# Turning q, k and features by row halves into two banks, and summing the tail's keys inside each step, in a Performer attention feeding two mixtures

## The chip, the cores and the metric

One core of one Trainium2 chip runs the whole program. The metric is the device time of one execution in microseconds (us), a median over runs. The engines are TensorE (PE, with its weight loads shown as PEld), VectorE (DVE), ScalarE (ACT), GpSimd (POOL) and SyncE (SP, which issues transfers). Each works through its own instructions in order and waits for others by semaphores.

## The reference

Random-feature attention over 2 batches, 8 heads, 576 tokens and 64 columns a head, then two mixtures of dense products whose cost dwarfs it:

```python
def phi(x):
    proj = np.einsum('bhsd,md->bhsm', x, omega)          # 128 features
    h = proj - np.sum(x * x, axis=-1, keepdims=True) / 2.0
    h = h - np.max(h, axis=-1, keepdims=True)
    return np.exp(h) / np.sqrt(m)
q_p, k_p = phi(q_s), phi(k_s)
kv = np.einsum('bhsm,bhsd->bhmd', k_p, v)
z = np.sum(k_p, axis=2)
num = np.einsum('bhsm,bhmd->bhsd', q_p, kv)
den = np.einsum('bhsm,bhm->bhs', q_p, z)[..., None] + 1e-06
x = (num / den)                                           # to 1152 x 512
for e in range(4):                                        # first mixture
    out += p[:, e:e + 1] * (np.maximum(x @ w1[e], 0.0) @ w2[e])
h = out @ w_in                                            # second mixture
return (h * np.cos(h)) @ w_out
```

## The kernel before

Attention is worked off in steps `s`, one for each of the 8 pairs of heads of one batch. A step has 512 tokens a head: four tokens lie on each of the 128 partitions, so a head is four tiles of 128 tokens. The last 64 tokens of every head and batch are kept apart as the "tail" (`kL`, `qL`, `veL`, features `phiL`): batch 0 on partitions 0 to 63, batch 1 on 64 to 127.

The steps are a software pipeline, written out by hand in the loop over `s`; there is no scheduler, so each engine's order is the order of the code. In one step TensorE does, in this order: the rest of `nums(s-2)` (tile `num`: features of q times kv, 128x64 weights, two column halves side by side); `kv_of(s-1)` (features of k times v, written into a free corner of a `num` bank, so its rows read `num<-ve,phk`); `turn_ahead(s)` (turns q of step s and k of step s+1, `tp_q` and `tp_k`, four 128x128 turns each); `turn_phi(s-1)` (turns the features of q, `tq`, eight turns); the products with omega for q and for k (`pj_q`, `pj_k`, in two row halves side by side); and the turn of the finished attention rows (`tx`). From step 6 on quanta of the dense products (`g`) are put between `tx` and `num`. Everything after about 84 us is dense products.

VectorE copies `xT_q` and half of the turned features `pT` out of PSUM, takes the maxima of `pj` (`three_q`, `three_k`), divides (`rd`, `xs`) and adds the tail's part to kv (`kv<-num,kvL`, L1172). ScalarE copies `xT_k` and the other half of `pT` and does all exponentials (`phq`, `phk`, L1092). The tail's keys times values are made once, in step 1, by `kv_tail`: 32 small products in four banks (`kvL`), copied out by VectorE in four pieces of 128x260.

PSUM has eight banks, all from one pool. Tiles of a step reuse the banks of earlier ones: a product must wait until the readers of its bank's last tile are done. `pj_k` of a step waits in this way for the division and the kv addition of the same step.

Of the kernel before, what the change touches and what calls it, by code (L numbers as in the profile page):

```python
# [9 lines left out]
F32 = mybir.dt.float32  # L10
# [16 lines left out]
def performer_moe_kernel(ctx, tc, q, k, v, omega, probs, w1, w2, w_in, w_out, out):  # L27
    nc = tc.nc
# [921 lines left out]
    with tc.tile_pool(name="at1", bufs=1) as at1, tc.tile_pool(name="at2", bufs=2) as at2:  # L950
# [76 lines left out]
        def turn(nm, t, pieces=1):  # L1027

            n = R // pieces
            tps = []  # L1030
            for z in range(pieces):
                tp = bank(f"tp_{nm}_{z}")[:, : n * P]
                tps.append((slice(z * n * P, (z + 1) * n * P), tp))
                for i in range(n):
                    nc.tensor.transpose(
                        tp[:, i * P : (i + 1) * P], t[:, 2 * (z * n + i) : 2 * (z * n + i) + 2, :], ident
                    )

            def copy(x=None, x2=None, act=nm[0] == "k"):
                if x is None:  # L1040
                    x = at2.tile([P, R * P], F32, tag=f"xT{nm[0]}", name=f"xT_{nm}")
                for z, (c, tp) in enumerate(tps):
                    if act and z == 0:
                        nc.scalar.activation(x[:, c], tp, ACTF.Copy)
                    else:
                        nc.vector.tensor_copy(out=x[:, c], in_=tp)
                    if x2 is not None:
                        nc.scalar.activation(x2[:, c], tp, ACTF.Square)
                return x

            return copy

        def features(nm, turned, phi, squares=None, shift_later=False):
# [35 lines left out]
            for g, pj in enumerate(pjs):  # L1089
                for i in range(4):  # L1090
                    ix = g + 2 * i
                    nc.scalar.activation(  # L1092
                        phi[:, ix, :], pj[:, i * M : (i + 1) * M], ACTF.Exp, bias=nb[:, ix : ix + 1]
                    )
                yield

        def divide(nm, parts):

# [39 lines left out]
        kvL = at1.tile([P, H, B, D + 1], F32, name="kvL")  # L1138
# [6 lines left out]
        def kv_tail(phi):  # L1145
            for z in range(2):
                hs = range(z * H // 2, (z + 1) * H // 2)
                sums_ = [
                    bank(f"kvL_{z}_{b}")[:, : H // 2 * (D + 1)].rearrange("p (h e) -> p h e", e=D + 1) for b in range(B)
                ]  # L1150
                for n, h in enumerate(hs):
                    for c in (slice(0, P // 2), slice(P // 2, P)):
                        for b in range(B):
                            bl = slice(b * L, (b + 1) * L)
                            nc.tensor.matmul(
                                sums_[b][c, n, :], phi[bl, h, c], veL[bl, h, :], start=True, stop=True
                            )
                for b in range(B):
                    nc.vector.tensor_copy(out=kvL[:, hs.start : hs.stop, b, :], in_=sums_[b])

        def kv_of(i):
            b, hp = pairs[i]
            ve, phk = ves[i % 2], phks.pop(i)
            kvp = room.pop() if room else bank(f"kv_{i}")
            kvp = kvp[:, 4 * (D + 1) : 6 * (D + 1)].rearrange("p (h e) -> p h e", h=2)
            for h in range(2):
                for r in range(R):
                    column_halves(
                        kvp[:, h, :], phk[:, h * R + r, :], ve[:, h * R + r, :], r == 0, r == R - 1
                    )  # L1170
            yield
            nc.vector.tensor_tensor(out=kv[hp][:, :, b, :], in0=kvp, in1=kvL[:, 2 * hp : 2 * hp + 2, b, :], op=ALU.add)  # L1172

        pTs = {}
        room = []

        def turn_phi(i):
            phq = phqs[i]
            for h in range(2):
                tp = bank(f"tq_{i}_{h}")  # L1180
                for r in range(R):
                    nc.tensor.transpose(tp[:, r * P : (r + 1) * P], phq[:, h * R + r, :], ident)
                pT = at2.tile([P, R * P], F32, tag=f"pT{h}", bufs=1, name=f"pT_{i}_{h}")
                if h == 0 and i:
# [3 lines left out]
                pTs[i, h] = pT  # L1188

        def nums(i):  # L1190
            b, hp = pairs[i]
            xss[i] = xs = at2.tile([P, R, 2, D], F32, tag="xs", bufs=1, name=f"xs_{i}")
            parts = []
            for h in (1, 0):
                pT = pTs.pop((i, h))
                num = bank(f"num_{i}_{h}")
                for r in range(R):
                    column_halves(
                        num[:, r * (D + 1) : (r + 1) * (D + 1)], pT[:, r * P : (r + 1) * P], kv[hp][:, h, b, :]
                    )  # L1200
# [4 lines left out]
            divide(i, parts)  # L1205

        def tail_turn_phi():
            phq = phqs[NPR]
            for g in range(2):
                tp = bank(f"tqL_{g}")  # L1210
                for i in range(4):
                    nc.tensor.transpose(tp[:, i * P : (i + 1) * P], phq[:, 4 * g + i, :], ident)
                pT = at2.tile([P, R * P], F32, tag=f"pT{g}", bufs=1, name=f"pTL_{g}")
                if g == 0:
                    nc.scalar.activation(pT, tp, ACTF.Copy)
                else:
                    nc.vector.tensor_copy(out=pT, in_=tp)
                pTs[NPR, g] = pT

        def tail_nums():  # L1220
            xss[NPR] = xs = at2.tile([P, NP, 2, D], F32, tag="xs", bufs=1, name="xsL")
            parts = []
            for z in range(2):
                num = bank(f"numL_{z}")
                for n in range(H // 2):
                    hp, h = divmod(z * H // 2 + n, 2)
                    for b in range(B):
                        bl = slice(b * L, (b + 1) * L)
                        nc.tensor.matmul(
                            num[bl, n * (D + 1) : (n + 1) * (D + 1)],  # L1230
                            pTs[NPR, z][:, n * P + b * L : n * P + (b + 1) * L],
                            kv[hp][:, h, b, :], start=True, stop=True,
                        )
                parts.append((num, xs.rearrange("p n h d -> p (n h) d")[:, z * 4 : z * 4 + 4, :]))
# [54 lines left out]
            return qL if s == NPR else qts[s]  # L1289

        def turn_ahead(s, act=True):
            splits = []
            if s <= NPR:
                splits.append((("q", s), turn(f"q{s}", q_of(s))))
            if s + 1 < NPR:
                splits.append((("k", s + 1), turn(f"k{s + 1}", kts[s + 1])))
# [52 lines left out]
        for s in range(NPR + 3):  # L1349
# [4 lines left out]
            else:  # L1354
# [111 lines left out]
```

## Time and profile before

| | |
|---|---|
| median of 3 runs | 640.69 us (640.3 to 640.7) |
| the profiled execution's own time | 640.93 us |
| its span, first to last instruction | 639.2 us |
| TensorE busy | 633.7 us, 99% |
| VectorE / ScalarE / GpSimd busy | 76% / 55% / 27% |
| granted clock of TensorE | 1.00 throughout |

TensorE is named busy nearly all of the time, but its matmuls are pipelined and their ends are modelled, so "busy" also covers short waits between them. The shares of the other engines are averages over two unlike parts: 84 us with attention, and 555 us of dense products.

### The profile page before, as it was taken

How to read it: one execution, taken by the hardware profiler on the slowest of the kernel's cores; microseconds unless marked ns; L12 is line 12 of the kernel's file. 1: busy time of each engine (PE TensorE's matmuls, PEld its weight loads, DVE VectorE, ACT ScalarE, POOL GpSimd, SP SyncE). 2: the span in 40 equal slices, each digit the busy share in tenths (PEclk: the TensorE clock that was granted, in tenths of full speed). 3: DMA queues.
4: the chain of work that ended last, by engine and by line, in shares of the span. 5: the costliest groups of instructions: out<-in, count | busy, mean ns of one | idle time of the engine just before them, and what ended most of it. 6: DMA issues, size and time to landing. Idle time of an engine off the chain costs nothing.

```text
span 639.2 us, 10046 instructions
## 1 busy us (share of the span) xinstructions
PE 633.7 (99%) x3751; PEld 538.0 (84%) x3751; DVE 488.5 (76%) x878; ACT 352.8 (55%) x686; POOL 173.8 (27%) x218
## 2 busy tenths in 40 slices
PE   8999999999999999999999999999999999999997
PEld 7999989988888888888888888888888888888887
DVE  5998578789688688598687697699698772697842
ACT  6898664365346454354443455544457973476821
POOL 7899752033332333323333232310000000000000
PEclk9999999999999999999999999999999999999999
DMA  7645430313446434347424445401250002500111
GB/s 166 188 118 149 133 100 31 102 67 131 133 148 200 146 106 143 128 148 217 134 98 132 138 130 209 132 35 70 85 208 33 2 0 91 239 1 2 49 50 49
DMA packets 55440, 70.95 MB, mean 111 GB/s; under 512 B 15200, under 2 KB 40032, under 8 KB 55392
## 3 DMA queue, kind: packets, MB, share of 16 engines
q1 hardware_dynamic: 46800, 40.92, 20.5%
q0 software_dynamic: 8448, 29.37, 13.5%
q8 instruction: 29, 0.48, 0.3%
q14 instruction: 19, 0.16, 0.1%
q10 hardware_dynamic: 144, 0.03, 0.0%
HBM read 55.36 MB, written 14.94 MB: 110 GB/s over the span
## 4 chain that ended last, share of the span: by engine, by line
PE 97%; DVE 1%; DMA 1%; SPq 0%; issue 0%; DVEq 0%
PE g L779 46%; PE g_odd L585 4%; PE g L549 3%; PE g_1c L549 2%; PE g_0a L549 2%; PE g_3a L549 2%; PE g_2a L549 2%; PE g_1a L549 2%; PE g_3c L549 2%; PE g_2c L549 2%; PE g_0c L549 2%; PE num L1143 2%; PE pj_q L1062 1%; PE g_0d L549 1%; PE g_0b L549 1%; PE g_3e L549 1%
## 5 line engine op out<-in xcount | busy, mean ns | idle before, releaser
L749 ACT ACTIVATE sth<-h 128x512 fp32r<-128x512 f32 (+1 forms) x111 | 60.3, 555 | 80.3 <-PE g L779 66.4
L258 POOL TENSOR_TENSOR c<-c 128x512 uint32<-128x512 uint32 x32 | 46.9, 1467 | 84.6 <-issue 34.2
L752 DVE SCALAR_TENSOR_TENSOR stl<-h,sth 128x512 fp32r<-128x512 f32 (+1 forms) x72 | 48.9, 694 | 27.1 <-ACT sth L749 26.9
L779 PE MATMUL g<-v3h,sth 128*128 128x512 f32 (+1 forms) x110 | 42.9, 390 | 0.0
L779 PE MATMUL g<-v0h,sth 128*128 128x512 f32 (+1 forms) x110 | 42.7, 388 | 0.0
L779 PE MATMUL g<-v1h,sth 128*128 128x512 f32 (+1 forms) x110 | 42.7, 388 | 0.0
L779 PE MATMUL g<-v2h,stl 128*128 128x512 f32 (+1 forms) x110 | 42.5, 387 | 0.0
L779 PE MATMUL g<-v2h,sth 128*128 128x512 f32 (+1 forms) x110 | 42.5, 386 | 0.0
L779 PE MATMUL g<-v0h,stl 128*128 128x512 f32 (+1 forms) x110 | 42.4, 386 | 0.0
L779 PE MATMUL g<-v3l,sth 128*128 128x512 f32 (+1 forms) x110 | 42.4, 386 | 0.0
L779 PE MATMUL g<-v3h,stl 128*128 128x512 f32 (+1 forms) x110 | 42.4, 386 | 0.0
L779 PE MATMUL g<-v1h,stl 128*128 128x512 f32 (+1 forms) x110 | 42.4, 385 | 0.0
L779 PE MATMUL g<-v1l,sth 128*128 128x512 f32 (+1 forms) x110 | 42.4, 385 | 0.0
L779 PE MATMUL g<-v0l,sth 128*128 128x512 f32 (+1 forms) x110 | 42.4, 385 | 0.0
L779 PE MATMUL g<-v2l,sth 128*128 128x512 f32 (+1 forms) x110 | 42.4, 385 | 0.0
L293 DVE TENSOR_TENSOR stl<-h,sth 128x512 fp32r<-128x512 f32 (+1 forms) x39 | 22.8, 594 | 19.3 <-ACT sth L749 19.1
L451 DVE SCALAR_TENSOR_TENSOR c<-c 128x512 f32<-128x512 f32 (+1 forms) x38 | 25.0, 662 | 11.9 <-ACT c L449 11.7
L448 ACT ACTIVATE c<-h 128x512 f32<-128x512 f32 x32 | 19.9, 621 | 19.8 <-DVE h L626 19.8
L805 DVE SCALAR_TENSOR_TENSOR acc<-g,pn,acc 128x512 f32<-128x512 f32 x27 | 20.1, 745 | 6.7 <-PE g L779 6.7
L779 PEld LDWEIGHTS g<-v2h,stl 128*128 128x128 f32 x110 | 20.7, 188 | 4.5 <-DVE stl L752 0.4
L779 PEld LDWEIGHTS g<-v0h,stl 128*128 128x128 f32 x110 | 20.7, 188 | 4.3 <-DVE stl L752 0.2
L779 PEld LDWEIGHTS g<-v3h,stl 128*128 128x128 f32 x110 | 20.7, 188 | 4.2
(427 smaller groups left out, 1880.5 us busy)
## 6 DMA issues: line engine op xcount, KB each, us to landing
rv<-in_moe_w_dram SPq DMA_DIRECT2D x16, 512.0 KB, 3.9
c<-in_moe_w_in_dram POOLq DMA_DIRECT2D x16, 512.0 KB, 4.1
c<-in_moe_w_out_dram POOLq DMA_DIRECT2D x16, 512.0 KB, 3.9
kt<-in_k_dram SPq DMA_DIRECT2D x8, 256.0 KB, 3.5
qt<-in_q_dram SPq DMA_DIRECT2D x8, 256.0 KB, 4.0
ve<-in_v_dram SPq DMA_DIRECT2D x16, 128.0 KB, 4.0
ra_2as<-in_moe_w_dram SPq DMA_DIRECT2D x8, 256.0 KB, 3.3
out_dram<-acc SPq DMA_DIRECT2D x7, 256.0 KB, 2.3
```

The source lines that it names most:

```text
L258: nc.gpsimd.tensor_tensor(out=total, in0=t, in1=lw, op=ALU.add)
L293: nc.vector.tensor_tensor(out=dst, in0=x, in1=y, op=ALU.subtract)
L448: nc.scalar.activation(vv, src, ACTF.Copy, bias=0.25, scale=INV_2PI)
L451: nc.vector.scalar_tensor_tensor(out=vv, in0=kk, scalar=ROUND, in1=vv, op0=ALU.subtract, op1=ALU.subtract)
L549: nc.tensor.matmul(dst, x[:, o], y[:, kk], start=start and n == 0, stop=stop and n == 3 * kn - 1, skip_group_check=reopen,)
L585: nc.tensor.matmul(g, x[:, kk], w[:, :, :, kk, :], start=n == 0, stop=n == 3 * KD - 1)
L749: nc.scalar.activation(hi, src, ACTF.Relu if self.e < E else ACTF.Copy)
L752: nc.vector.scalar_tensor_tensor(out=to, in0=src, scalar=0.0, in1=hi.bitcast(F32), op0=ALU.max, op1=ALU.subtract)
L779: nc.tensor.matmul(g, x, y[:, o : o + w], start=n == 0, stop=n == 3 * FT - 1)
L805: nc.vector.scalar_tensor_tensor(out=acc[t], in0=src, scalar=p_, in1=acc[t], op0=ALU.mult, op1=ALU.add)
L1062: nc.tensor.matmul(pj[:, i * M : (i + 1) * M], x_[r, c], y[r, :], start=z == 0, stop=z == (squares is not None),)
L1143: nc.tensor.matmul(dst[c], weights[:, c], moving, start=start, stop=stop)
```

## The change

Four things change. `turn_ahead` and `turn_phi` no longer turn whole 128x128 tiles. The new `row_halves` turns partitions 0 to 63 and 64 to 127 of each tile by two instructions (64 rows by 128 columns of weights, 64 moving columns) that write into two banks; each bank then holds one row half of all tiles, so both q and k, and both heads, need both banks' copies. One copy is VectorE's, the other ScalarE's (both VectorE's where only q is turned). `kv_tail` and its copies are gone: `kv_of` adds the tail's product for a head as a fifth term behind the four of the step, so that kv's addition becomes a plain copy. The exponentials of the tail's features are reordered so that heads 0 and 1 come first. `nums` and `tail_nums` take their weights from the new layout.

```diff
+        def row_halves(dsts, srcs):
+            for n, src in enumerate(srcs):
+                for z, dst in enumerate(dsts):
+                    r = slice(z * D, (z + 1) * D)
+                    nc.tensor.transpose(dst[:, n * D : (n + 1) * D], src[r], ident[r, r])
...
                 for r in range(R):
-                    column_halves(
-                        kvp[:, h, :], phk[:, h * R + r, :], ve[:, h * R + r, :], r == 0, r == R - 1
-                    )
-            yield
-            nc.vector.tensor_tensor(out=kv[hp][:, :, b, :], in0=kvp, in1=kvL[:, 2 * hp : 2 * hp + 2, b, :], op=ALU.add)
+                    column_halves(kvp[:, h, :], phk[:, h * R + r, :], ve[:, h * R + r, :], r == 0, False)
+                column_halves(kvp[:, h, :], phiL[bl, n, :], veL[bl, n, :], False, True)
+            yield
+            nc.vector.tensor_copy(out=kv[hp][:, :, b, :], in_=kvp)
...
         def turn_phi(i):
-            phq = phqs[i]
-            for h in range(2):
-                tp = bank(f"tq_{i}_{h}")
-                for r in range(R):
-                    nc.tensor.transpose(tp[:, r * P : (r + 1) * P], phq[:, h * R + r, :], ident)
+            tps = [bank(f"tq_{i}_{z}") for z in range(2)]
+            row_halves(tps, [phqs[i][:, n, :] for n in range(2 * R)])
...
-            for key, split in splits:
-                turned[key] = split(act=act and key[0] == "k")
+            n = len(parts) * R
+            tps = [bank(f"tp_{s}_{z}")[:, : n * D] for z in range(2)]
+            row_halves(tps, [t[:, 2 * i : 2 * i + 2, :] for _, t in parts for i in range(R)])
+            x = at2.tile([P, 2 * R * P], F32, tag="xT", name=f"xT_{s}")
+            to = x[:, : n * P].rearrange("p (i z t) -> p i z t", z=2, t=D)
+            for z, tp in enumerate(tps):
+                src = tp.rearrange("p (i t) -> p i t", t=D)
+                if z and act and n > R:
+                    nc.scalar.activation(to[:, :, z, :], src, ACTF.Copy)
+                else:
+                    nc.vector.tensor_copy(out=to[:, :, z, :], in_=src)
...
                 if s == 1:
                     turn_phi(0)
-                    kv_tail(phiL)
                     next(kvs, None)
```

How TensorE's order moves from kv to the turns, in the middle of step 3. Before (`ve` and `phk` are v and the features of k, `qt` and `kt` q and k as loaded, `ident` the unit matrix):

```order
L1143 MATMUL num_1_633<-ve_131,phk_432 64x65 [waits DMAHW0_49]
L1143 MATMUL num_1_633<-ve_131,phk_432 64x65 x7
L1143 MATMUL num_1_633<-ve_131,phk_432 64x65 [waits DMAHW1_49]
L1143 MATMUL num_1_633<-ve_131,phk_432 64x65 x7
L1035 MATMUL tp_q_0_677<-ident,qt_3_504 128x128 [waits DMAHW7_49]
L1035 MATMUL tp_q_0_677<-ident,qt_3_504 128x128 x3
L1035 MATMUL tp_k_0_682<-ident,kt_0_502 128x128 [waits DMAHW6_49,DVE_49,Activation_49]
L1035 MATMUL tp_k_0_682<-ident,kt_0_502 128x128 x3
```

The same place on TensorE in the changed kernel, up to the first turns:

```order
L1148 MATMUL num_1_630<-ve_131,phk_410 64x65 [waits DMAHW0_49]
L1148 MATMUL num_1_630<-ve_131,phk_410 64x65 x7
L1148 MATMUL num_1_630<-veL,phiL 64x65 x2
L1148 MATMUL num_1_630<-ve_131,phk_410 64x65 [waits DMAHW1_49]
L1148 MATMUL num_1_630<-ve_131,phk_410 64x65 x7
L1148 MATMUL num_1_630<-veL,phiL 64x65 x2
L1143 MATMUL tp_0_678<-ident,qt_3_482 128x64 [waits DMAHW7_49,PE_49]
L1143 MATMUL tp_1_679<-ident,qt_3_482 128x64 [waits DVE_49,Activation_49]
```

Each head's eight products are now followed by two of the tail, which use 64 rows of weights where their neighbours use 128; and the turns of q alternate between two banks, as those of k behind them do.

VectorE in step 1, before (`pT` are the turned features of q, `kvL` the tail's part, `three` the maxima):

```order
L1187 COPY pT_1_388<-tq_1_383 128x512 [waits PE_49]
L1159 COPY kvL<-kvL_0_390 128x4x65 [waits PE_49]
L1159 COPY kvL<-kvL_1_391 128x4x65 [waits PE_49]
L1159 COPY kvL<-kvL_0_410 128x4x65 [waits PE_49]
L1159 COPY kvL<-kvL_1_411 128x4x65 [waits PE_49]
L1172 TENSOR_TENSOR kv_138<-kv_359,kvL 128x2x65 [waits DVE_49]
L1069 TENSOR_REDUCE three_q_455<-x_q_287 128x8 [waits Pool_49]
```

The same place on VectorE in the changed kernel:

```order
L1175 COPY pT_0_404<-tq_0_386 128x512 [waits PE_49]
L1175 COPY pT_1_406<-tq_1_387 128x512 [waits PE_49]
L1162 COPY kv_138<-kv_365 128x2x65
L1069 TENSOR_REDUCE three_q_433<-x_q_286 128x8 [waits Pool_49]
L1075 TENSOR_REDUCE three_q_433<-pj_q_0_412 128x4 [waits PE_49]
```

The four copies of `kvL` are gone, and what was an addition to kv is a copy.

## Rows read from the trace of the kernel before

**Rows 1.** The page, part 1: busy us (share of the span) x instructions.

```profile
PE 633.7 (99%) x3751; PEld 538.0 (84%) x3751; DVE 488.5 (76%) x878; ACT 352.8 (55%) x686; POOL 173.8 (27%) x218
```

**Rows 2.** Busy time of each engine by stage; window, its length, then each engine.

```profile
core 0: us, PE busy (x) PEld busy (x) DVE busy (x) ACT busy (x) POOL busy (x), PEclk, DMA share, GB/s
...
21.60:49.40 27.80, 27.80 (x475) 25.20 (x472) 26.86 (x87) 26.65 (x89) 25.12 (x36) 1.00 0.53 145
49.40:84.00 34.60, 34.55 (x410) 32.16 (x409) 22.34 (x67) 26.47 (x71) 29.12 (x32) 1.00 0.42 121
84.00:639.00 555.00, 551.81 (x2562) 462.98 (x2558) 425.29 (x688) 286.23 (x486) 102.77 (x120) 1.00 0.32 106
```

**Rows 3.** The chain that ended last, one step: start us, us, what.

```profile
28.37 0.59 PE tp_q L1035 x4
28.96 0.44 PE tp_k L1035 x4
29.40 0.90 PE tq L1182 x8
30.30 1.09 PE pj_q L1062 x16
31.39 1.06 PE pj_k L1062 x16
32.45 0.59 PE tx L1116 x4
33.04 2.02 PE num L1143 x64
```

**Rows 4.** Timeline, one turn of the loop: start us, us, engine, line, out<-in.

```profile
29.10 0.68 DVE L1046 COPY xT_q<-tp_q 128x512 f32<-128x512 f32 x1
...
30.38 0.76 DVE L1108 TENSOR_TENSOR xs<-num,rd 128x256 f32<-128x256 f32 x2
...
31.05 0.28 DVE L1172 TENSOR_TENSOR kv<-num,kvL 128x130 f32<-128x130 f32 x1
...
31.29 1.16 PE L1062 MATMUL pj_k<-ws,xT_k 64*128 64x128 f32 x16
...
32.38 0.66 PE L1116 MATMUL tx<-ident,xs 128*128 128x128 f32 x4
...
32.97 1.15 PE L1143 MATMUL num<-kv,pT 128*64 128x65 f32 x32
...
33.95 1.10 PE L1143 MATMUL num<-ve,phk 128*64 128x65 f32 x32
...
34.99 0.66 PE L1035 MATMUL tp_q<-ident,qt 128*128 128x128 f32 x4
...
35.70 0.68 DVE L1046 COPY xT_q<-tp_q 128x512 f32<-128x512 f32 x1
```

**Rows 5.** Timeline: the kv addition and `pj_k`, three loops later.

```profile
51.29 0.28 DVE L1172 TENSOR_TENSOR kv<-num,kvL 128x130 f32<-128x130 f32 x1
...
51.53 1.16 PE L1062 MATMUL pj_k<-ws,xT_k 64*128 64x128 f32 x16
```

**Rows 6.** Timeline of step 1.

```profile
16.30 2.17 ACT L1092 ACTIVATE phk<-pj_k,nb_k 128x128 f32<-128x128 f32 x8
...
17.32 1.43 DVE L1159 COPY kvL<-kvL 128x260 f32<-128x260 f32 x4
```

**Rows 7.** Timeline: the first `num` behind step 1.

```profile
19.62 1.15 PE L1143 MATMUL num<-kv,pT 128*64 128x65 f32 x32
```

**Rows 8.** Timeline, two weight loads of `tp_q`: all four, then the second alone.

```profile
41.81 0.42 PEld L1035 LDWEIGHTS tp_q<-ident,qt 128*128 128x128 f32 x4
...
41.87 0.14 PEld L1035 LDWEIGHTS tp_q<-ident,qt 128*128 128x128 f32 x1
```

**Rows 9.** Timeline of step 7, where only q is turned.

```profile
60.09 0.69 DVE L1046 COPY xT_q<-tp_q 128x512 f32<-128x512 f32 x1 [2.38 <-PE tp_q L1035]
...
62.07 0.66 PE L1116 MATMUL tx<-ident,xs 128*128 128x128 f32 x4
```

More of the change, by code (lines that the diff above doesn't have):

```diff
@@ L1040, in copy @@
                 if x is None:
-                    x = at2.tile([P, R * P], F32, tag=f"xT{nm[0]}", name=f"xT_{nm}")
+                    x = at2.tile([P, R * P], F32, tag=f"xT{nm[0]}", bufs=1 + (nm[0] == "k"), name=f"xT_{nm}")
                 for z, (c, tp) in enumerate(tps):
@@ L1088, in features @@
             yield
[L1089 to L1093, printed above, removed]
-                    )
-                yield
+            order = [g + 2 * i for g in range(2) for i in range(R)]
+            if squares is not None:
+                order.insert(1, order.pop(R))
+            for ix in order:
+                i, g = divmod(ix, 2)
+                nc.scalar.activation(
+                    phi[:, ix, :], pjs[g][:, i * M : (i + 1) * M], ACTF.Exp, bias=nb[:, ix : ix + 1]
+                )
         def divide(nm, parts):
@@ L1143, in column_halves @@
                 nc.tensor.matmul(dst[c], weights[:, c], moving, start=start, stop=stop)
[L1145 to L1159, printed above, removed]
         def kv_of(i):
@@ L1165, in kv_of @@
             kvp = kvp[:, 4 * (D + 1) : 6 * (D + 1)].rearrange("p (h e) -> p h e", h=2)
+            bl = slice(b * L, (b + 1) * L)
             for h in range(2):
+                n = 2 * hp + h
                 for r in range(R):
-                    column_halves(
-                        kvp[:, h, :], phk[:, h * R + r, :], ve[:, h * R + r, :], r == 0, r == R - 1
-                    )
+                    column_halves(kvp[:, h, :], phk[:, h * R + r, :], ve[:, h * R + r, :], r == 0, False)
+                column_halves(kvp[:, h, :], phiL[bl, n, :], veL[bl, n, :], False, True)
             yield
-            nc.vector.tensor_tensor(out=kv[hp][:, :, b, :], in0=kvp, in1=kvL[:, 2 * hp : 2 * hp + 2, b, :], op=ALU.add)
+            nc.vector.tensor_copy(out=kv[hp][:, :, b, :], in_=kvp)
         pTs = {}
@@ L1177, in turn_phi @@
         def turn_phi(i):
-            phq = phqs[i]
-            for h in range(2):
-                tp = bank(f"tq_{i}_{h}")
-                for r in range(R):
-                    nc.tensor.transpose(tp[:, r * P : (r + 1) * P], phq[:, h * R + r, :], ident)
-                pT = at2.tile([P, R * P], F32, tag=f"pT{h}", bufs=1, name=f"pT_{i}_{h}")
-                if h == 0 and i:
+            tps = [bank(f"tq_{i}_{z}") for z in range(2)]
+            row_halves(tps, [phqs[i][:, n, :] for n in range(2 * R)])
+            for z, tp in enumerate(tps):
+                pT = at2.tile([P, R * P], F32, tag=f"pT{z}", bufs=1, name=f"pT_{i}_{z}")
+                if z and i:
                     nc.scalar.activation(pT, tp, ACTF.Copy)
@@ L1187, in turn_phi @@
                     nc.vector.tensor_copy(out=pT, in_=tp)
-                pTs[i, h] = pT
+                pTs[i, z] = pT
         def nums(i):
@@ L1194, in nums @@
             for h in (1, 0):
-                pT = pTs.pop((i, h))
                 num = bank(f"num_{i}_{h}")
                 for r in range(R):
-                    column_halves(
-                        num[:, r * (D + 1) : (r + 1) * (D + 1)], pT[:, r * P : (r + 1) * P], kv[hp][:, h, b, :]
-                    )
+                    for z in range(2):
+                        nc.tensor.matmul(
+                            num[z * D : (z + 1) * D, r * (D + 1) : (r + 1) * (D + 1)],
+                            pTs[i, z][:, (h * R + r) * D : (h * R + r + 1) * D],
+                            kv[hp][:, h, b, :], start=True, stop=True,
+                        )
                 parts.append((num, xs[:, :, h, :]))
@@ L1207, in tail_turn_phi @@
         def tail_turn_phi():
[L1208 to L1218, printed above, removed]
+            turn_phi(NPR)
         def tail_nums():
@@ L1230, in tail_nums @@
                             num[bl, n * (D + 1) : (n + 1) * (D + 1)],
-                            pTs[NPR, z][:, n * P + b * L : n * P + (b + 1) * L],
+                            pTs[NPR, b][:, (z * 4 + n) * L : (z * 4 + n + 1) * L],
                             kv[hp][:, h, b, :], start=True, stop=True,
@@ L1291, in turn_ahead @@
         def turn_ahead(s, act=True):
-            splits = []
-            if s <= NPR:
-                splits.append((("q", s), turn(f"q{s}", q_of(s))))
+            parts = [(("q", s), q_of(s))] if s <= NPR else []
             if s + 1 < NPR:
-                splits.append((("k", s + 1), turn(f"k{s + 1}", kts[s + 1])))
-            for key, split in splits:
-                turned[key] = split(act=act and key[0] == "k")
+                parts.append((("k", s + 1), kts[s + 1]))
+            if not parts:
+                return
+            n = len(parts) * R
[3 more added lines that the diff above has]
+            to = x[:, : n * P].rearrange("p (i z t) -> p i z t", z=2, t=D)
+            for z, tp in enumerate(tps):
+                src = tp.rearrange("p (i t) -> p i t", t=D)
[3 more added lines that the diff above has]
+                    nc.vector.tensor_copy(out=to[:, :, z, :], in_=src)
+            for j, (key, _) in enumerate(parts):
+                turned[key] = x[:, j * R * P : (j + 1) * R * P]
         def k_features(s, shift_later=False):
```

1 line of the change is left out of this document (removed).

## The prediction

> **What bounds the kernel now.** I read the page first: TensorE is named busy for 99% of the span [rows 1]. The busy times by stage say where the change can matter: behind 84 us TensorE has 551.81 us of work in 555, and between 49.4 and 84 us 34.55 in 34.60, so whatever the attention steps shift arrives at the end undiminished [rows 2]. From 21.6 to 49.4 us it is otherwise: TensorE 27.80, VectorE 26.86, ScalarE 26.65, GpSimd 25.12 of 27.80. Four engines are all but full, so a saving on one of them is not yet a saving of time. The chain that ended last names TensorE alone there [rows 3], and taken at its word the turns (0.59 + 0.44 + 0.90 us a step) are on the path. But the chain follows one releaser where two come together. The timeline shows the second: VectorE's copy `xT_q` at 29.10 starts an unbroken series on VectorE (copy, small reductions, `xs`, the kv addition) that ends at 31.05 + 0.28 = 31.33, and `pj_k` starts at 31.29. Then TensorE runs `tx`, `num`, kv and `tp_q` with no more than the changes of shape between them, and `xT_q` of the next step starts at 35.70, when `tp_q` at 34.99 + 0.66 has ended [rows 4]. That is a closed loop of 6.60 us: 2.19 on VectorE, 1.09 for `pj_k`, 0.59 `tx`, 0.98 `num`, 1.04 kv, 0.71 for the turn of q and its way to VectorE. Three loops later the kv addition ends at 51.57 and `pj_k` starts at 51.53 [rows 5]. So it is tight throughout: `pj_k` needs banks that the division and the kv addition free. What matters in steps 2 to 6 is what the change does to this loop, not to TensorE's work.
>
> **Prices.** A turn of 128x128 costs 0.44 / 4 = 0.11 us. `tp_q`, the same four turns behind a change of tile shape, costs 0.59, and `tx` 0.59 too: 0.15 us for each change of shape. The 32 pairs of column halves of `num` and kv (64 records, two to a matmul) cost 2.02 less one change, 1.87 / 32 = 0.058 us a pair [rows 3].
>
> **The turns.** A pair of row halves moves 64 columns in each half, about what a pair of `num` moves (65), so I price it at 0.058; the bounds are that and 0.11, if the two halves gain nothing on a whole turn. A second weight load of a turn started 0.06 us after the first [rows 8], which sits at the lower bound. For that lower bound against the upper one: the Trainium skill ("TensorE: Matmul & The Clock Gate", section LDWEIGHTS) says that a weight load takes P / 1.2 ns with P the columns, whatever the rows. By it the 128 columns of a half would take an estimated 107 ns, a pair would cost what a turn costs, and the sum below would rise by the 2.8 us of the second rival; the 0.06 us disagrees, and is what I go by.
>
> In the loop the turns gain nothing. Before, VectorE waited for four turns (0.44); now each of the two banks is ready only when all eight pairs of q and k are done, 8 x 0.058 = 0.46: +0.02. The 0.4 us saved on `tq` and the change of shape that falls away ahead of `pj_q` lie beside VectorE's series and ScalarE's copy, which `pj_q` now needs as well.
>
> **The tail inside kv.** For each head two matmuls are added, two pair times, 2 x 0.058 = 0.12; four pairs a step, 0.23. They hold 64 rows of weights among neighbours with 128, so the shape changes into them and out of them for both heads; the last change out was there already. Three changes are new, 3 x 0.15 = 0.45. Together +0.68 a step, on TensorE between `num` and the turns, inside the loop, with nothing beside it. No row shows a change from 128x64 to 64x64; its bounds are 0 and the 0.15 of the changes in [rows 3], and I take 0.15 because it is what both of those cost. Behind this stands the Trainium skill ("TensorEngine Tiling (Array Packing)", section Key Properties): a change of the tiling mode, not of the tile alone, drains TensorE, and it lists 128x64 and 64x64 as different modes. The rows agree for the shapes that they hold; no row has this one.
>
> The kv addition (0.28) becomes a copy. Four copies of 260 took 1.43, 0.36 each [rows 6], so 130 should take between half of that and 0.28: I take 0.23, -0.05.
>
> **Step 1.** The 1.43 us of copies leave VectorE, which is full there, and with them the 32 products of `kv_tail`. But `num` at 19.62 [rows 7] cannot come forward by more than about 1.1: one of its two banks is freed by the exponentials of k's features, which end at 16.30 + 2.17 = 18.47 [rows 6] and do not depend on what changes. Bounds 0 and -1.1; I take -1.0, since TensorE itself would be there by then (the tail's first products wait for two exponentials, which the new order of the features puts first).
>
> **Steps 7 to 9.** TensorE is the bound [rows 2]. Steps 7 and 8 pay the tail's +0.68 each. In step 7 `tx` waits for the series behind `xT_q` [rows 9]: four pairs instead of four turns give back 0.21, two copies of 256 columns instead of one of 512 (0.36 each against 0.69) take 0.03. I count -0.2 for step 7 and -0.1 for step 8. The tail's turn in step 9 saves 0.42 and pays two changes of shape, 0.30: -0.1.
>
> **Sum.** Step 1: -1.0. Steps 2 to 6: 5 x (0.68 + 0.02 - 0.05) = +3.25. Steps 7 and 8: 1.36 - 0.3 = +1.06. Step 9: -0.1. Together +3.2. The profiled execution took 640.93, its span 639.2 and 1.7 around it that doesn't change; the median of the runs is 0.24 lower. 640.93 + 3.2 = 644.1, against the median 640.69 + 3.2 = 643.9. With 0 to -1.1 for step 1 and 0.10 to 0.15 for each of the 21 changes of shape, this case alone spans 642.7 to 644.9.
>
> **Rivals.** First, not slower: going between 128x64 and 64x64 costs nothing, since both write 64 columns side by side. Then 21 x 0.15 = 3.15 falls away and the time is 640.7, no change that can be measured (0.2%, 1.3 us, is about what a measurement of this kernel tells from none). It decides from 0.06 us a change downward, where the sum drops under 1.3. Against it: both changes of shape that can be read off [rows 3] cost the same 0.15, though they come from different shapes (128x64 and 64x128). Second, the change does not do what it says: the halves do not run beside each other, or each is held up by its 128 columns of weights, and a pair costs 0.11. Then the loop's turns take 8 x 0.052 = 0.42 more, 2.1 in steps 2 to 6, with 0.3 in steps 7 and 8 and 0.4 in step 9: 646.7. Against it: the 0.06 us of [rows 8]. Third, faster: the loop through VectorE has slack that the timeline doesn't show, and TensorE's own work decides. Then a step saves 16 x 0.052 = 0.83 on turns and 0.15 on the shape ahead of `pj_q` and pays 0.68: -0.3, five times -1.5; steps 7 and 8 -0.1 each, step 9 -0.1, step 1 -1.1: 637.8. It decides where `pj_k` has 0.95 us (0.65 + 0.3) to spare behind VectorE; [rows 4, 5] leave it none.
>
> **How the numbers follow.** Chances: the forecast 0.62, free changes of shape 0.14, halves without gain 0.12, slack 0.12. Slower by over 0.2%: the forecast and the second rival, 0.74. Within 0.2%: most of the first rival and the shallow end of the third, 0.12. Faster: the rest, 0.14. The forecast's own range holds too little, so the range reaches down to the first rival and up to just short of the second: 640.4 to 646.4.
>
> **What would show it.** Right: the loop from one `xT` copy to the next at about 7.25 us instead of 6.6; kv between `num` and the turns at about 1.7 instead of 1.04, with idle ahead of each tail piece; sixteen row-half turns in about 0.6; `pj_k` still starting where the kv copy ends; the first dense quantum of step 6 about 2.2 later. Wrong: tail pieces that follow their neighbours with no gap; turns at over 0.8 for sixteen; or `pj_k` starting clear of the kv copy.

## The result, and the profile after

The changed kernel takes 644.22 us (median of 6 runs, 643.4 to 644.7) against 640.7 (640.3 to 640.9): a ratio of 1.0054, 95% interval 1.0042 to 1.0067. The profiled execution took 644.21, its span is 642.4 against 639.2. The forecast was 643.9.

The page, part 1, of the changed kernel (answers to [rows 1]):

```profile
PE 634.0 (99%) x3879; PEld 536.9 (84%) x3879; DVE 487.9 (76%) x876; ACT 354.0 (55%) x686; POOL 174.0 (27%) x218
```

Nothing shows here: TensorE has 128 more instructions and 0.3 us more busy time. The stages say more. Windows of the changed kernel; each ends at about the same work as its row in [rows 2], the first begins at the same time:

```profile
core 0: us, PE busy (x) PEld busy (x) DVE busy (x) ACT busy (x) POOL busy (x), PEclk, DMA share, GB/s
21.60:51.50 29.90, 27.98 (x566) 24.44 (x565) 26.45 (x85) 26.13 (x84) 27.04 (x38) 1.00 0.55 152
51.50:87.00 35.50, 34.23 (x464) 31.27 (x462) 21.61 (x69) 26.78 (x71) 26.69 (x28) 1.00 0.32 99
87.00:642.00 555.00, 551.86 (x2562) 463.02 (x2558) 426.53 (x688) 286.34 (x486) 103.37 (x121) 1.00 0.32 106
```

The first stage ends 2.1 us later, and TensorE, busy for 27.80 of 27.80 before, now stands for 1.9 of 29.90. The dense stretch has 551.86 of work, 551.81 before. So nearly the whole loss lies ahead of 87 us. One turn of the loop, from the timeline of the changed kernel in step 3 and the first part of step 4 (answers to [rows 4]):

```profile
29.03 0.69 DVE L1287 COPY xT<-tp 128x512 f32<-128x512 f32 x1 [0.53 <-PE tp L1143]
...
33.89 0.64 PE L1148 MATMUL num<-ve,phk 128*64 128x65 f32 x16
...
34.46 0.33 PE L1148 MATMUL num<-veL,phiL 64*64 64x65 f32 x4
...
34.72 0.69 PE L1148 MATMUL num<-ve,phk 128*64 128x65 f32 x16
...
35.34 0.33 PE L1148 MATMUL num<-veL,phiL 64*64 64x65 f32 x4
...
35.60 0.47 PE L1143 MATMUL tp<-ident,qt 64*128 64x64 f32 x8
...
35.90 0.41 PE L1143 MATMUL tp<-ident,kt 64*128 64x64 f32 x8
...
36.15 0.67 PE L1143 MATMUL tq<-ident,phq 64*128 64x64 f32 x16
...
36.35 0.69 DVE L1287 COPY xT<-tp 128x512 f32<-128x512 f32 x1 [0.63 <-PE tp L1143]
...
37.16 1.00 PEld L1062 LDWEIGHTS pj_q<-ws,xT 64*128 64x128 f32 x16 [0.48 <-ACT xT L1285]
...
37.64 0.76 DVE L1109 TENSOR_TENSOR xs<-num,rd 128x256 f32<-128x256 f32 x2
...
38.31 0.28 DVE L1162 COPY kv<-num 128x130 f32<-128x130 f32 x1
...
38.45 0.72 PEld L1062 LDWEIGHTS pj_k<-ws,xT 64*128 64x128 f32 x9 [0.29 <-DVE xs L1109]
```

From kv's first product to the first turn it takes 35.60 - 33.89 = 1.71, before 1.04 [rows 4]. Behind each tail piece the next work starts 0.26 us later, for two pairs. Eight turns of tiles (sixteen row halves) take 36.15 - 35.60 = 0.55, four pairs of k 0.25, a pair 0.06. And where the lines of [rows 4] have no bracket, three waits of step 4 now stand in brackets: VectorE for the turns (0.63), TensorE for ScalarE's copy of `xT` ahead of `pj_q` (0.48) and for `xs` ahead of `pj_k` (0.29). Ahead of `pj_k` the wait is not the same in every step. In steps 4 and 5 it is for `xs`; in steps 2, 3 and 6 it is for ScalarE's exponentials of k's features (`phk`, 0.46, 0.39 and 0.39), so in these steps the loop runs from the copy of `xT` over VectorE's `nb_k` and these exponentials to `pj_k`. Step 3, from the timeline of the changed kernel:

```profile
31.23 0.97 PEld L1062 LDWEIGHTS pj_k<-ws,xT 64*128 64x128 f32 x16 [0.39 <-ACT phk L1094]
```

Step 1 of the changed kernel, from its timeline (answers to [rows 6, 7]):

```profile
14.28 0.33 PE L1148 MATMUL kv<-veL,phiL 64*64 64x65 f32 x4 [0.55 <-ACT phiL L1094]
...
15.87 2.23 ACT L1094 ACTIVATE phk<-pj_k,nb_k 128x128 f32<-128x128 f32 x8
...
18.21 1.15 PE L1186 MATMUL num<-kv,pT 128*64 128x65 f32 x32
```

`num` starts 1.41 earlier. Further on, the copies of `xT` in steps 6, 7 and 8 and the first product behind the attention (answers to [rows 9] and to 49.33, 60.09, 69.63 and 84.20 before):

```profile
51.58 0.69 DVE L1287 COPY xT<-tp 128x512 f32<-128x512 f32 x1 [0.92 <-PE tp L1143]
...
62.82 0.76 DVE L1287 COPY xT<-tp 128x256 f32<-128x256 f32 x2 [3.43 <-PE tp L1143]
...
72.71 0.76 DVE L1287 COPY xT<-tp 128x256 f32<-128x256 f32 x2 [0.75 <-PE tp L1143]
...
87.20 0.50 PE L779 MATMUL g<-v0h,sth 128*128 128x512 f32 x1
```

Read as lateness against before this is the whole account: -1.41 at `num` of step 1, +2.25 in step 6, +2.73 in step 7, +3.08 in step 8, +3.00 at the dense products, +3.3 at the end (the medians differ by 3.5).

### The profile page after: what moved, and what is told of

Same layout as the page of the kernel before. It is cut to its first block, busy times and chain, and to the rows that moved or that the text cites. A ratio compares the mean times of both kernels' runs of the same rounds, so it can differ in the third digit from the quotient of the medians.

```text
span 642.4 us, 10310 instructions
## 1 busy us (share of the span) xinstructions
PE 634.0 (99%) x3879; PEld 536.9 (84%) x3879; DVE 487.9 (76%) x876; ACT 354.0 (55%) x686; POOL 174.0 (27%) x218
## 4 chain that ended last, share of the span: by engine, by line
PE 94%; DVE 3%; ACT 1%; issue 1%; DVEq 0%; ACTq 0%
PE g L779 44%; PE g_odd L585 4%; PE g L549 3%; PE g_1c L549 2%; PE g_0a L549 2%; PE g_3a L549 2%; PE g_2a L549 2%; PE g_1a L549 2%; PE g_2c L549 2%; PE g_3c L549 2%; PE g_0c L549 2%; PE num L1148 2%; PE num L1186 1%; PE pj_k L1062 1%; PE g_0d L549 1%; PE g_0b L549 1%
```

## The experiments

Each median is over 4 to 11 executions. The first columns are read from the one execution of each kernel that was profiled, from the starts of VectorE's copy of `xT` (of q alone where it is a copy of its own) in steps 2 to 6: four loops. "Dense" is the start of the product that stands at 87.20 above. The start of the first `num` behind step 1 varied within 17.7 to 18.6 in the eleven kernels without the tail's sums in step 1 and within 19.35 to 19.62 in the three with them, so loops are compared and not absolute starts.

| kernel | loops, us | four loops | dense | median, us | ratio to before, 95% |
|---|---|---|---|---|---|
| before | 6.77 6.60 6.81 6.82 | 27.00 | 84.20 | 640.7 to 641.0 | |
| changed | 7.39 7.32 7.62 7.61 | 29.94 | 87.20 | 644.22 | 1.0054 (1.0042 to 1.0067) |
| e1 turns alone | 6.77 6.64 7.06 6.94 | 27.41 | 84.33 | 642.09 | 1.0018 (1.0009 to 1.0026) |
| e2 tail alone | 7.33 7.28 7.50 7.51 | 29.62 | 87.51 | 643.60 | 1.0040 (1.0026 to 1.0053) |
| e3 tail over 128 rows | 6.95 6.88 7.17 7.18 | 28.18 | 84.62 | 641.07 | 1.0005 (0.9996 to 1.0014) |
| e4 tails together | 7.24 7.18 7.47 7.46 | 29.35 | 86.44 | 642.73 | 1.0028 (1.0017 to 1.0039) |
| e5 tq twice | 7.59 7.52 7.62 7.61 | 30.34 | 87.30 | 645.90 | 1.0081 (1.0067 to 1.0095) |
| e6 whole turns, 128 rows | 6.89 6.82 7.06 7.07 | 27.84 | 83.97 | 640.73 | 0.9998 (0.9989 to 1.0007) |
| e7 whole turns of q, k | 7.34 7.26 7.97 7.96 | 30.53 | 87.48 | 644.72 | 1.0062 (1.0048 to 1.0076) |
| e8 kv addition twice | 7.09 6.92 7.00 7.00 | 28.01 | 85.02 | 641.50 | 1.0011 (1.0002 to 1.0020) |
| e9 second head late, 128 rows | 10.27 10.22 10.25 10.23 | 40.97 | 99.58 | 655.70 | 1.0232 (1.0218 to 1.0246) |
| e10 second head late | 9.00 10.34 10.39 10.41 | 40.14 | 99.66 | 657.82 | 1.0258 (1.0242 to 1.0274) |
| e11 whole turns of features | 7.39 7.32 7.41 7.41 | 29.53 | 87.00 | 644.29 | 1.0055 (1.0043 to 1.0068) |
| e12 second head early | 7.72 7.53 7.53 7.52 | 30.30 | 85.78 | 642.98 | 1.0033 (1.0021 to 1.0045) |

**One part alone: e1 and e2.** e1 is the changed kernel with `kv_tail` and the addition back (these lines undone), e2 the kernel before with these alone:

```diff
-                    column_halves(kvp[:, h, :], phk[:, h * R + r, :], ve[:, h * R + r, :], r == 0, r == R - 1)
+                    column_halves(kvp[:, h, :], phk[:, h * R + r, :], ve[:, h * R + r, :], r == 0, False)
+                column_halves(kvp[:, h, :], phiL[bl, n, :], veL[bl, n, :], False, True)
...
-            nc.vector.tensor_tensor(out=kv[hp][:, :, b, :], in0=kvp, in1=kvL[:, 2 * hp : 2 * hp + 2, b, :], op=ALU.add)
+            nc.vector.tensor_copy(out=kv[hp][:, :, b, :], in_=kvp)
...
-                    kv_tail(phiL)
```

> The turns by row halves alone; the tail's part of kv is made once in step 1 and added, as before (q0's and k0's copies share buffers of later steps to make room). Theory (a loop through VectorE sets steps 2 to 6, and eight row-half pairs of q and k, 0.46 us, replace four whole turns, 0.44 us, in it): no gain in the loop (+0.1 in five steps), -0.4 in steps 7 to 9: 640.4 us, 639.9 to 640.9. Rival A (TensorE's own work decides): 0.98 us a step less, five times, and -0.4: about 635.4. Rival B (the copies that now hold q and k together start later or end later than the one of q did, which is why a loop of the changed kernel takes 7.3 to 7.6 us, not 7.25): 0.1 to 0.35 a step more, 640.8 to 642.0.

> The tail inside kv alone (with the new order of the exponentials of its features); turns are whole 128x128 ones, as before. Theory: 7 steps of +0.68 us, less the 1.4 us that step 1 gives back in the changed kernel: 640.7 + 4.8 - 1.4 = 644.1 us (643.5 to 644.6), about what the whole change takes. Rival A (the added products hide beside other engines' work and the turns are what costs): 640.7 less the 1.4 us of step 1, about 639.3 to 640.7.

e2 took 643.60: the tail is nearly all of the loss, with 29.62 - 27.00 = 2.62 in four loops, 0.66 each on the mean. e1, at 642.09, missed the theory's 640.4. It gains nothing in the loop, so TensorE's own work does not decide (635.4 is refuted); it even loses 0.41 in four loops, nearly all of it in the last two (0.25 and 0.12). Rival B was right that something is lost there, though not by the copies of `xT`; e7 and e11 show what it is. At the dense products e1 is only 0.13 late, at the end 1.15. The rest arises at two places behind the attention, 0.4 near 96.6 and 0.66 here. TensorE in the dense stretch of e1, from its timeline:

```profile
100.15 0.50 PE L779 MATMUL g<-v2h,stl 128*128 128x512 f32 x1 [0.57 <-DVE stl L752]
```

VectorE's `stl` comes too late, and TensorE waits 0.57 us; the same product has no such wait before. ScalarE's split of the weights `v3h`, which stands ahead of the activations that `stl` needs, waited in e1 for its load until 81.19, and until 80.06 before. That the one makes the other is read from the order of the work and was not varied by itself, and why the load landed later is open. It need not belong to the turns: the profiled execution of e3 (below) has the same late split (81.23) and the same wait (0.53 at 100.13), and took 642.07, 1.0 above e3's median.

**The price of a change of shape: e3 and e4.** e3 keeps the number of products and their columns, but takes all 128 rows, with zeros for the other batch (to make room, the copies of k's first turns get one buffer instead of two):

```diff
-        veL = at1.tile([P, H, D + 1], F32, name="veL")
+        veLs = [at1.tile([P, H, D + 1], F32, name=f"veL{b}") for b in range(B)]
+        for b, t in enumerate(veLs):
+            nc.vector.memset(t[(1 - b) * L : (2 - b) * L], 0.0)
...
-                column_halves(kvp[:, h, :], phiL[bl, n, :], veL[bl, n, :], False, True)
+                column_halves(kvp[:, h, :], phiL[:, n, :], veLs[b][:, n, :], False, True)
```

e4 sums the tail of head 0 behind its own products and that of head 1 ahead of them, so that both stand together:

```diff
+                if h == 1:
+                    column_halves(kvp[:, h, :], phiL[bl, n, :], veL[bl, n, :], True, False)
                 for r in range(R):
...
-                column_halves(kvp[:, h, :], phiL[bl, n, :], veL[bl, n, :], False, True)
+                if h == 0:
+                    column_halves(kvp[:, h, :], phiL[bl, n, :], veL[bl, n, :], False, True)
```

> The changed kernel with the tail's products over all 128 rows: v of each batch's tail in a copy of its own with zeros in the other batch's rows, so that features of all 128 rows are the weights and no product changes the tile's shape. As many products of the same 65 columns. Theory (three new changes of shape a step at 0.15 us): 7 steps x 0.45 = 3.15 less, 641.1 us (640.5 to 641.7). Rival (changes between 128x64 and 64x64 cost nothing and the products themselves or the longer loop of the copies cost): 644.2, no change.

> The changed kernel with the tail's products of both heads next to each other between the two heads' own products: two new changes of tile shape a step instead of three, all else the same. Theory: 7 steps x 0.15 = 1.05 less, 643.2 us (642.8 to 643.6). Rival (changes of shape cost nothing): 644.2.

The loops came as the theory says: e3 took 641.07, its loops are 0.44 shorter each (0.44, 0.44, 0.45, 0.43); e4's loops are 0.15 shorter each (0.15, 0.14, 0.15, 0.15), and its 642.73 is a little under the range. One change of shape fewer is worth 0.15, three are worth 0.44. The same place in e3, from its timeline in step 3:

```profile
33.87 0.29 PE L1150 MATMUL num<-veL,phiL 128*64 128x65 f32 x4
...
33.99 0.64 PE L1150 MATMUL num<-ve,phk 128*64 128x65 f32 x16
...
34.45 0.29 PE L1150 MATMUL num<-veL,phiL 128*64 128x65 f32 x4
...
34.67 0.46 PE L1145 MATMUL tp<-ident,qt 64*128 64x64 f32 x8
...
35.42 0.69 DVE L1288 COPY xT<-tp 128x512 f32<-128x512 f32 x1 [0.20 <-PE tp L1145]
```

Behind the first tail piece the next products start after 0.12, two pairs and no more, where the changed kernel needs 0.26; and the second head's own products take 0.46 up to their tail piece, there 0.62. The change into the turns (34.45 to 34.67) was there before.

**Work added beside the loop and in it: e5 and e8.** e5 is the changed kernel with the features of q turned twice in steps 2 to 6, e8 the kernel before with its kv addition made twice there:

```diff
             row_halves(tps, [phqs[i][:, n, :] for n in range(2 * R)])
+            if 1 <= i <= 5:
+                row_halves(tps, [phqs[i][:, n, :] for n in range(2 * R)])
```

```diff
-            nc.vector.tensor_tensor(out=kv[hp][:, :, b, :], in0=kvp, in1=kvL[:, 2 * hp : 2 * hp + 2, b, :], op=ALU.add)
+            for _ in range(1 + (1 <= i <= 5)):
+                nc.vector.tensor_tensor(
+                    out=kv[hp][:, :, b, :], in0=kvp, in1=kvL[:, 2 * hp : 2 * hp + 2, b, :], op=ALU.add
+                )
```

> The changed kernel, whose features of q are turned twice in steps 2 to 6: eight more row-half pairs, 8 x 0.058 = 0.46 us of TensorE a step, right behind the first ones, where TensorE of the changed kernel then waits 0.5 us ahead of pj_q for the copies of xT. Theory (the loop through VectorE decides, and TensorE's work beside the copies is free): no change, 644.2 us (643.9 to 644.7). Rival (TensorE's own work decides): 5 x 0.46 = 2.3 more, 646.5.

> The kernel before with VectorE's addition to kv made twice in steps 2 to 6 (the same sum written again): 0.28 us more on VectorE ahead of pj_k in each of five loops, and no more work for TensorE. Theory (the loop through VectorE is tight): 5 x 0.28 = 1.4 more than before, 642.2 us against 640.8 (641.8 to 642.6). Rival (slack behind VectorE; TensorE's own work decides): no change, 640.8.

Up to the dense products e5 is as expected: with eight more pairs the loops of steps 4 and 5 keep their 7.62 and 7.61, those of steps 2 and 3 grow by 0.20, far less than the 0.46 added; the dense products start 0.10 later (step 1 began 0.32 earlier in this run). The time of 645.90 lies outside the theory's range and nearer to the rival's 646.5, but the rival's reason is not seen: the profiled execution loses the rest in two waits for VectorE's `stl`, 0.58 at 102.81 (the changed kernel has 0.22 at this product) and this one, from the timeline of e5:

```profile
427.67 0.50 PE L779 MATMUL g<-v0h,stl 128*128 128x512 f32 x1 [0.78 <-DVE stl L752]
```

Why `stl` is late there is not settled. e8 says that VectorE is tight, though its 641.50 is under the theory's range: the second addition costs all of its 0.33 us (0.61 - 0.28) in two loops (+0.32) and 0.19 and 0.18 in two more, +1.01 over four, and nothing in step 6, where I had counted it too; with a step 1 that began 0.19 earlier that is the +0.8 at the dense products. But it also corrects me. The kv addition and `pj_k` of step 2 in e8, from its timeline:

```profile
24.17 0.61 DVE L1173 TENSOR_TENSOR kv<-num,kvL 128x130 f32<-128x130 f32 x2
...
24.41 0.52 PEld L1062 LDWEIGHTS pj_k<-ws,xT_k 64*128 64x128 f32 x8
```

`pj_k` starts while the second addition still runs to 24.78, so here it doesn't wait for kv. Nor for `xs`, which has ended at 24.25: the last thing that it waits for is ScalarE's fourth exponential of k's features, to 24.36. So it is in steps 2, 3 and 6 of the kernel before and of the changed one too. In steps 4 and 5 it is otherwise: there the first products of `pj_k` need `xs`, and the next ones, in the other bank, the kv addition. Step 4 of e8, from its timeline:

```profile
38.26 0.30 PEld L1062 LDWEIGHTS pj_k<-ws,xT_k 64*128 64x128 f32 x2
...
38.76 0.96 PEld L1062 LDWEIGHTS pj_k<-ws,xT_k 64*128 64x128 f32 x14 [0.20 <-DVE kv L1173]
```

What the addition lengthens is VectorE's own series from one `xT` copy to the next, which is unbroken in all four loops of e8. Before, it was unbroken in the first two; at the end of the other two VectorE waited 0.13 for the turns, and these grow by that much less than 0.33.

**Which turns lose: e7 and e11.** e7 has `turn_ahead` as before, e11 has `turn_phi`, `nums` and the tail's turn as before; the rest is the changed kernel. Their cores:

```diff
-            row_halves(tps, [t[:, 2 * i : 2 * i + 2, :] for _, t in parts for i in range(R)])
...
+            for key, split in splits:
+                turned[key] = split(act=act and key[0] == "k")
```

```diff
-            row_halves(tps, [phqs[i][:, n, :] for n in range(2 * R)])
...
+                for r in range(R):
+                    nc.tensor.transpose(tp[:, r * P : (r + 1) * P], phq[:, h * R + r, :], ident)
```

> The changed kernel with whole turns of q and k, as before (a bank and a copy for each), and the features still turned by row halves. Theory (the loop needs the turn of q alone, 4 x 0.11 = 0.44 us against eight pairs of 0.058 = 0.46, and both copies for pj_q): 0.02 to 0.1 us a loop less, 643.7 us (643.5 to 644.2). Rival (row halves of q and k do save time): 4 x 0.052 us a tile for eight tiles, 0.42 a step, five steps: 646.3.

> The changed kernel with whole turns of the features, head by head, as before; q and k still by row halves. Then num's first head needs VectorE's copy of pT alone, and ScalarE's later copy hides under it. Theory (in the changed kernel num waits for ScalarE's copy, 0.1 us in each of the loops of steps 4 and 5 and 0.05 in the others): 0.3 less, 643.9 us (643.5 to 644.3), with loops of 7.3, 7.3, 7.5 and 7.5 us. Rival (row halves of the features save TensorE 8 x 0.052 = 0.42 a step in the loop): 5 x 0.42 more, 646.3.

e11 has 7.41 and 7.41 in the last two loops, 0.2 less each than the changed kernel, where the theory asked for 0.1; the first two are the changed kernel's own, where it asked for 0.05. Its time is the same within the measurement. e7 went against the theory: its last two loops take 7.97 and 7.96, 0.46 longer than e2's, which differs from it in the features alone. Both point to one wait. ScalarE's copy of `pT` and `num` in e7, from its timeline:

```profile
39.57 0.66 ACT L1173 ACTIVATE pT<-tq 128x512 f32<-128x512 f32 x1
...
39.66 0.33 PE L1186 MATMUL num<-kv,pT 128*64 128x65 f32 x2
...
40.28 0.39 PE L1186 MATMUL num<-kv,pT 128*64 128x65 f32 x6 [0.28 <-ACT pT L1173]
```

With whole turns the first head's eight products need VectorE's copy alone, and ScalarE's ends under them. With row halves every second product needs ScalarE's bank: after the first one (two records) TensorE stands until 40.23. So the turns of the features by row halves cost 0.2 to 0.46 us in these two loops. In steps 4 and 5, and not in 2 and 3, ScalarE also splits a weight ahead of its exponentials (`w02h`, 1.05 us), which fits its copy being late there; this was not varied.

**Without shape changes and without row halves: e6.** e2 with the edit of e3, the candidate for the best of both:

```diff
-                column_halves(kvp[:, h, :], phiL[bl, n, :], veL[bl, n, :], False, True)
+                column_halves(kvp[:, h, :], phiL[:, n, :], veLs[b][:, n, :], False, True)
```

> The kernel before with the tail inside kv over all 128 rows (zeros in the other batch's rows of v) and whole turns. Theory: the kernel with the tail alone (643.6) less 7 x 0.45 us of changes of shape: 640.5 us (639.9 to 641.1), about what the kernel before takes, since 7 steps of four pairs (0.23 us) and the 1.1 us that step 1 gives nearly cancel. Rival (what step 1 gives stays in the end, and the four pairs hide): 639.4.

640.73, no difference from before: its four loops are 0.84 longer (0.21 each on the mean, about the four pairs), and step 1 gives that back. No version of these parts beat the kernel before.

**Kv's second head behind the turns: e9, e10, e12.** The second head's products of kv move behind the turns of q and k in steps 2 to 6, to take them off the way to the copy of `xT` (e9 is this edit in e3, e10 in the changed kernel):

```diff
             for h in range(2):
                 n = 2 * hp + h
+                if h and 1 <= i <= 5:
+                    yield
```

> The kernel with the tail over 128 rows (641.1), and in steps 2 to 6 the second head's products of kv, with its tail's, put behind the turns of q and k instead of ahead of them: 0.35 us leave the way from num to the copy of xT, and two changes of shape (0.30) come to TensorE beside the copies. Theory (the loop through VectorE decides until VectorE's own series is unbroken; xT's copy can start at most 0.2 to 0.25 earlier, when xl has ended): 4.5 loops x 0.22 = 1.0 less, 640.1 us (639.7 to 640.8). Rival (TensorE's own work decides): 5 x 0.30 = 1.5 more, 642.6.

> The same move in the changed kernel itself, with its 64-row pieces: 0.65 us of kv (0.35 and two changes of shape) leave the way from num to the copy of xT; one more change of shape, 0.15. Theory: the loop shortens until TensorE's own order is as long, which from the trace of the changed kernel is about 0.35 a loop: 644.2 - 4.5 x 0.35 = 642.6 us (642.0 to 643.3). Rival (TensorE's own work decides already): 5 x 0.15 = 0.75 more, 645.0.

Both missed their forecasts by some 15 us, in a way that neither theory held. In e9's and e10's programs these products stand behind the division of the same step, which reads their bank (kv lies in a corner of a `num` bank), and so they wait for it. Step 2 of e9, from its timeline and, below, its windows of 1 us:

```profile
21.96 0.76 DVE L1111 TENSOR_TENSOR xs<-num,rd 128x256 f32<-128x256 f32 x2
...
22.43 1.13 PE L1150 MATMUL num<-ve,phk 128*64 128x65 f32 x16 [2.19 <-DVE xs L1111]
```

```profile
21.00:22.00 1.00, 0.00 (x0) 0.00 (x0) 0.90 (x8) 0.92 (x4) 0.83 (x3) 1.00 0.57 136
22.00:23.00 1.00, 0.56 (x10) 0.57 (x12) 0.71 (x2) 1.00 (x6) 0.92 (x2) 0.66 0.08 17
23.00:24.00 1.00, 1.00 (x22) 0.88 (x20) 0.17 (x1) 0.85 (x4) 0.92 (x2) 0.50 0.00 0
...
25.00:26.00 1.00, 1.00 (x16) 1.00 (x16) 0.75 (x2) 0.50 (x1) 0.92 (x2) 0.63 1.04 368
26.00:27.00 1.00, 1.00 (x22) 0.97 (x18) 0.70 (x2) 0.00 (x0) 0.92 (x2) 1.00 0.79 210
```

TensorE stands 2.19 us behind `xs`, and then the granted clock (third column from the right) is 0.50 until between 25 and 26. Each of e9's loops is 3.0 to 3.4 us longer than e3's. The first loop of e10 tells the wait from the clock. The wait of its step 2, from its timeline, and its window of 20 to 30 us:

```profile
22.44 0.69 PE L1148 MATMUL num<-ve,phk 128*64 128x65 f32 x16 [1.87 <-DVE xs L1109]
```

```profile
20.00:30.00 10.00, 7.29 (x156) 6.34 (x154) 7.97 (x25) 7.68 (x27) 8.95 (x14) 1.00 0.60 162
```

TensorE stands 1.87 us there, the clock stays at 1.00, and the loop takes 9.00, 1.6 more than the changed kernel's; in e10's other three the clock falls behind a wait of about 1.8, and they take 2.8 to 3.0 more. e12 puts the same products into the program ahead of the division:

```diff
                     turn_ahead(s)
+                    if 2 <= s <= 6:
+                        next(kvs)
```

> The same move as in the run with 655.7 us, but the second head's products stand in the program between the turns and the division, so that they wait for no read of their bank by the division (there TensorE stood 1.8 to 1.9 us behind xs in every loop). Theory (that wait, and the lower clock that followed it, made all of the loss; the loop through VectorE shortens by 0.2 to 0.25 us once kv's second head is off it): 641.1 - 1.0 = 640.1 us (639.6 to 640.9), clock 1.00, loops of 6.7 to 6.95. Rival A (TensorE's own work decides, two changes of shape more): 642.6. Rival B (the turns of q and k can't start earlier, since a bank is freed only by the features of q): no gain, 641.1 to 642.0.

The wait for the division and the lower clock are gone (643.0 instead of 655.7, clock 1.00 in all 10-us windows up to 84 us), but the loops are 7.5 to 7.7, not 6.7 to 6.95, and longer than e3's by 0.34 to 0.77. The time comes near rival A's 642.6, but TensorE stands still in every loop, so its work isn't what decides. Rival B named the wait, though with another bank and without a price. The turns of step 3 in e12, from its timeline:

```profile
34.31 0.74 DVE L1134 TENSOR_TENSOR xl<-tx,xh 128x384 fp32r<-128x384 f32 x2
...
35.20 0.43 PE L1145 MATMUL tp<-ident,qt 64*128 64x64 f32 x7 [1.01 <-DVE xl L1134]
...
35.89 0.69 DVE L1290 COPY xT<-tp 128x512 f32<-128x512 f32 x1 [0.84 <-PE tp L1145]
```

The first turn had started at 33.91, the second needs the other bank, and that is freed when VectorE has read `tx` out of it (`xl`, to 35.05). Row halves need both banks from the second instruction on.

## Why the prediction was right, step by step

**The loop** was right as the place, and its size nearly: +0.735 a loop (2.94 / 4) where +0.65 was forecast, and TensorE's saved work came to nothing (e1, e5).

**What frees `pj_k`'s banks** was wrong for the steps from which it was read. "`pj_k` needs banks that the division and the kv addition free", as the description of the kernel before has it too, was taken from `pj_k` at 31.29 and 51.53, just ahead of the ends of two kv additions. In these steps (3 and 6), and in step 2, the wait that ends last is for the fourth of ScalarE's eight exponentials of k's features. From the timeline of the kernel before:

```profile
30.10 2.17 ACT L1092 ACTIVATE phk<-pj_k,nb_k 128x128 f32<-128x128 f32 x8
```

The fourth of the eight ends at 31.24, `pj_k` follows at 31.29, and the kv addition runs on to 31.33: that the two ends agree is chance. Only in steps 4 and 5 do `xs` and the kv addition come last (e8). The price of the tail doesn't hang on this, since kv lies on TensorE's part of the loop whatever frees the banks. And VectorE's series left next to no room in any case (e8).

**The tail inside kv**: +0.67 in kv (1.71 against 1.04) where 0.68 was forecast, and 0.66 a loop by e2. The 0.15 for a change between 128x64 and 64x64, which no row of before showed, is what e3 and e4 measured (0.44 / 3 and 0.15). Free changes, the first rival, are refuted.

By the Trainium skill ("TensorEngine Tiling (Array Packing)", section Key Properties) the change of mode drains TensorE; e3 and e4 agree that such a change costs time, and put 0.15 us on it here.

**The turns in the loop**: the pair was priced right (0.06 against 0.058), so halves without gain, the second rival, is refuted. The step that was mis-sized is "+0.02": e1 has +0.10 a loop. It named both copies that `pj_q` needs, but not that `num` now needs both copies of `pT` at once, ScalarE's included (e7's bracket).

The ground given for that price was half luck: the 0.06 of [rows 8] is the one short gap at the head of a tile, and the third and fourth loads there start 0.11 us after the ones before them, as whole turns do. The pairs' own 0.06 was measured only in the changed kernel, where the loads of the two halves start together.

By the Trainium skill's price for a weight load ("TensorE: Matmul & The Clock Gate", section LDWEIGHTS) a pair would have cost what a whole turn does. The traces agree for whole turns, whose loads start 0.11 us apart, and disagree for the pairs, which start 0.06 apart.

**The kv copy** took 0.28, as the addition did, not 0.23: -0.05 did not come.

**Step 1**: `num` came 1.41 earlier, past the bound of -1.1, but 0.44 of that lies ahead of the change. The products `pj_kL`, which it leaves alone, start at 9.42 instead of 9.87 in the two profiled executions, and anywhere from 8.83 to 9.87 over all fourteen kernels. From there to `num` it takes 8.78 instead of 9.75: -0.97, where -1.0 was forecast. The bound named was the right one: `num` starts at 18.21, just behind the end of the exponentials of k's features at 15.87 + 2.23 = 18.10.

**Steps 7 to 9**: +0.48 in step 7, as forecast; +0.35 in step 8 (0.58); -0.08 to the dense products (-0.1).

So the mechanism was right, and that +3.3 between the two traces falls so close to +3.2 is luck, because the misses cancel: -0.4 from the earlier start ahead of step 1, +0.4 in steps 2 to 6 (3.66 against 3.25), -0.2 in step 8, and +0.3 in the dense stretch that was not forecast (with the wait of 0.22). The medians differ by 3.5.

**Slack**, the third rival, is refuted by e1 (no gain) and e8 (1.0 of the 1.3 added to four loops is paid). Shown, then: the tail's place in the loop and its changes of shape, and the wait for ScalarE's `pT`. Open: why `stl` in the dense stretch comes late in some executions, which is up to 1.7 us of time (e5).

## What to carry to other kernels

Price a small product by its neighbours as well as by its columns: here two pairs of 0.06 us cost 0.15 more for each change of tile shape into and out of them, and zeros that keep the shape took that away at once. Where work is split over two banks instead of one after the other, list who needs the first bank alone: that cover is lost, and the later of two copies becomes the wait. In a loop where several engines are within a few per cent of full, saved work on one of them can be worth nothing until the chain through the others is shorter; add a known piece of work to each of them in turn to see which one pays. And two times that agree in a timeline are not yet a wait: look for the last thing that the later one waits for, in more than one step.

## What was not expected of the hardware

The granted clock fell to 0.50, the 1.2 GHz level, behind waits of TensorE of 1.77 to 2.19 us (e9), and was back at 1.00 some 3 us later; sixteen row halves then took 1.12 us instead of 0.67, and each of e9's loops was over 3 us longer. But a wait of 1.87 us (e10, step 2) left the clock at 1.00. Reading 128x130 out of PSUM took VectorE 0.28 us as a copy and 0.28 as an addition. And in e1 a load of weights landed 1.1 us later than before, at 81 us, and TensorE waited for the work behind it 19 us later.
